# Computing, finishing and storing the last output tile of an MLP product in two column halves

## The chip, the cores and the metric

The kernel runs on one core of a Trainium2 chip. The metric is the device time of one execution in microseconds (us), the median over several executions. A profile's span is 2.1 to 2.2 us shorter than the time of the same execution (139.9 against 142.1 for the kernel before). Times inside an execution are counted from the start of that span.

## The reference, cut to what matters

```python
def _B_ref(x, w1, b1, w2, b2):
    h = _layernorm(x, axis=-1)
    u = jnp.einsum("bsd,sf->bdf", h, w1) + b1
    u = _gelu(u)
    y = jnp.einsum("bdf,fs->bds", u, w2) + b2          # the second MLP product
    return y.transpose(0, 2, 1)

h  = x + _A_ref(_layernorm(x), A_w_r, A_w_i)           # spectral filter, not touched here
h2 = h + _B_ref(_layernorm(h), B_w1, B_b1, B_w2, B_b2) # S = 2048, D = 512, F = 1376
```

The output has 2048 x 512 elements in bf16. The kernel makes it as 16 tiles of 128 x 512. Each tile needs 11 accumulating matmuls over F, one eviction by the vector engine (DVE) that adds the bias and `h`, and one store.

## The kernel before

The kernel is built by its own small scheduler: each operation is recorded with its dependences, ordered on its engine, and emitted with semaphores. Two parts matter. The first is the loop of the second product:

```python
for s2 in range(NS2):                                   # 16 tiles
    unit = PsumUnit("mm2", 1, early=True)
    for t in range(NFT):                                # 11 matmuls, the last with 96 rows
        Kt = NP if t < 10 else 96
        mm(..., lambda bank: ps[:, bank, :], W2[t][0:Kt, s2::16], GT[0:Kt, t, :], unit, ...)   # strided weights
    dst, bia, hs = OUT[:, s2, :], B2f[:, s2:s2 + 1], H[:, s2, :]
    K.op(f"fin{s2}", "dve", ... eng.scalar_tensor_tensor(dst, ps[:, bank, :], bia, hs, op0=ALU.add, op1=ALU.add), ...)
    dma(f"st_{s2}", out_psd[:, s2, :], dst, 1 << 17, ins=[dst], prio=9)
```

The second is where the instructions of each engine are emitted. `sp` is the sync engine, which issues all of the stores:

```python
def section(eng, sname=sname, ops=ops):
    last = {o.lane for o in ops[-4:]}
    for k, o in enumerate(ops):
        if sname == "sp" and k == len(ops) - 2:         # before the second-to-last DMA
            for lane in sorted(self.lane_count):
                if lane.startswith("dq") and lane not in last:
                    eng.wait_ge(sems[lane], lane_quantum(lane) * self.lane_count[lane])
        for lane, v in o.waits:
            eng.wait_ge(sems[lane], v * lane_quantum(lane))
        ins = o.emit(...)
        ...
    if sname == "sp":
        for lane in sorted(last):                       # the last four, at the end
            eng.wait_ge(...)
```

So before the second-to-last DMA of the sync engine, whichever that is, the program waits once for every DMA semaphore that is not one of the last four. The built program has 30 wait instructions there, most of them with two semaphores each. The Trainium skill describes such instructions ("Perfetto Trace Analysis", section "Identifying Dependency Chains"): an instruction that waits on several engines may have EventSemaphore instructions put in front of it. The trace has 30 such records in front of that store, 29 for the program's own waits and one with the store's wait for its eviction. I call them "the wait block".

## Time and profile before

| | kernel before |
|---|---|
| time, median | 141.94 us (141.81 to 142.0, 4 runs) |
| span of the profiled execution | 139.9 us |
| PE (matmul) busy | 122.4 us, 87% |
| last matmul over, last eviction begins | 136.74 us |
| last eviction | 0.75 us |
| last store issued, landed | 137.52, about 139.4 us |

The end of the chain of waits, the chain of work that ended last (start, duration, engine, tile or line, count):

```profile
51.34 85.38 PE ps L549 x424
136.72 0.02 issue
136.74 0.75 DVE OUT L820
```

From 51 us to the last matmul nothing but PE is on the path. Work on the tail can win at most the 3.2 us from 136.74 to the end. The timeline of the kernel before shows the evictions and stores of the last two tiles, with the store of tile 13 first (start, duration, engine, line, operation, and in brackets the engine's idle time and what ended it; SPq is the sync engine's queue):

```profile
132.76 0.33 SPq L544 DMA_DIRECT2D out_dram<-OUT  x1
...
134.36 0.75 DVE L820 SCALAR_TENSOR_TENSOR OUT<-ps,B2f,H 128x512 bf16<-128x512 f32 x1 [1.63 <-PE ps L549]
...
135.46 0.33 SPq L544 DMA_DIRECT2D out_dram<-OUT  x1
...
136.74 0.75 DVE L820 SCALAR_TENSOR_TENSOR OUT<-ps,B2f,H 128x512 bf16<-128x512 f32 x1 [1.63 <-PE ps L549]
...
137.52 0.33 SPq L544 DMA_DIRECT2D out_dram<-OUT  x1
```

The last store goes 0.03 us after its eviction ends (136.74 + 0.75 = 137.49). The store of tile 14 does not: its eviction ended at 134.36 + 0.75 = 135.11, and it went at 135.46, 0.35 us late. That small irregularity is the only sign of the wait block in the ordinary views. The raw records of the sync engine show what lies between the stores of tiles 13 and 14 (start and duration in us; this is not a view of the profile, and the comments are mine):

```
132.762 DMA   0.333     store of tile 13
133.146 EVSEM 0.017     first of 30 wait instructions
...                     (about 0.06 apart)
133.823 EVSEM 0.028
134.277 EVSEM 0.028     after a hole of 0.45
...                     (about 0.06 apart)
135.388 EVSEM 0.027     the last one
135.456 DMA   0.327     store of tile 14
```

All the semaphores in it except that of tile 14's eviction had been reached long before, so the block is not waiting for data until its very end, and even that wait (the last of the 30) finds its eviction finished. It takes 135.456 - 133.095 = 2.36 us merely to be executed. The gap between two stores is 2.38 us less the 0.33 us of an issue, so here it costs nearly nothing.

For the last store, the view of the output tile gives the time from issue to landing:

```profile
DMA to landing us min/median/max: 1.9/1.9/1.9
```

### The profile page before, as it was taken

The numbers are of one execution on the slowest core, as the hardware profiler recorded it, in microseconds if no ns is written. First come the engines' busy times: TensorE is split into PE (matmuls) and PEld (weight loads), VectorE is DVE, ScalarE is ACT, GpSimd is POOL, SyncE is SP. The second block draws the span as 40 slices with busy tenths as digits, with TensorE's granted clock in tenths as the row PEclk, the third lists the DMA queues.
The fourth block names the chain that finished last, engine by engine and source line by source line (L and its number), as shares of the span: only waits on it lengthen the run. The fifth ranks groups of instructions, "written<-read, shape, count | busy, mean of one in ns | idle before, by whom it ended". The sixth has DMA issues, their size and how long they took to land.

```text
span 139.9 us, 2050 instructions
## 1 busy us (share of the span) xinstructions
PE 122.4 (87%) x754; PEld 76.6 (55%) x754; DVE 81.3 (58%) x169; ACT 64.0 (46%) x138; POOL 18.1 (13%) x49
## 2 busy tenths in 40 slices
PE   0039779999994899999999999999999999999990
PEld 0026557677663666764444444445666666666660
DVE  0489966998597399999200779544452324242422
ACT  3699973767855599984100996533300000000000
POOL 0077700000000003667400000000000000000000
PEclk9999999999999999999999999999999999999999
DMA  4999999999999999500000000000012121212111
GB/s 125 353 391 403 343 356 335 424 415 428 422 288 348 418 274 363 205 0 0 0 5 0 0 0 0 0 0 0 0 42 75 37 75 37 75 42 75 37 49 68
DMA packets 12218, 22.77 MB, mean 163 GB/s; under 512 B 2640, under 2 KB 8784, under 8 KB 11440
## 3 DMA queue, kind: packets, MB, share of 16 engines
q1 hardware_dynamic: 11776, 21.33, 42.5%
q10 hardware_dynamic: 432, 1.31, 2.7%
q8 instruction: 6, 0.10, 0.3%
q14 instruction: 4, 0.03, 0.1%
HBM read 20.54 MB, written 2.10 MB: 162 GB/s over the span
## 4 chain that ended last, share of the span: by engine, by line
PE 75%; DVE 13%; ACT 4%; DMA 3%; POOL 2%; issue 1%; POOLq 0%
PE ps L549 75%; DVE V L712 5%; DMA X<-in_A_x_dram 3%; DVE st_94 L648 2%; POOL FS L657 2%; ACT JK L627 2%; ACT PQ L557 1%; DVE H L763 1%; DVE Y L558 1%; DVE OUT L820 1%; DVE PQ L558 1%; DVE st_101 L769 0%; ACT CS L557 0%; DVE mv_95 L650 0%; DVE FS L657 0%
## 5 line engine op out<-in xcount | busy, mean ns | idle before, releaser
L549 PE MATMUL ps<-HH,W_77 128*128 128x512 bf16 (+1 forms) x176 | 39.8, 379 | 0.2 <-DVE HH L783 0.2
L549 PEld LDWEIGHTS ps<-HH,W_77 128*128 128x128 bf16 (+1 forms) x176 | 17.6, 100 | 19.1 <-issue 0.4
L820 DVE SCALAR_TENSOR_TENSOR OUT<-ps,B2f,H 128x512 bf16<-128x512 f32 x16 | 12.0, 750 | 23.8 <-PE ps L549 23.8
L549 PE MATMUL ps<-FS,X 128*128 128x256 bf16 x64 | 9.4, 315 | 10.2 <-POOL FS L657 10.2
L549 PEld LDWEIGHTS ps<-FS,X 128*128 128x128 bf16 x64 | 6.7, 112 | 12.6 <-POOL FS L657 9.7
L763 DVE TENSOR_TENSOR H<-ps,X 128x512 bf16<-128x512 f32 x16 | 10.4, 675 | 2.2 <-PE ps L549 2.2
L549 PE MATMUL ps<-EM,V 128*128 128x128 bf16 x128 | 9.6, 220 | 1.6 <-DVE V L712 1.5
L557 ACT ACTIVATE PQ<-ps 128x512 bf16<-128x512 f32 x15 | 8.2, 598 | 6.0 <-PE ps L549 5.9
L712 DVE TENSOR_TENSOR V<-ps,Wr 128x1024 bf16<-128x1024 f32 x8 | 9.5, 1220 | 2.3 <-PE ps L549 2.3
L549 PE MATMUL ps<-EM,Y 128*128 128x256 bf16 x64 | 9.1, 273 | 1.3 <-DVE Y L558 1.0
L549 PEld LDWEIGHTS ps<-EM,V 128*128 128x128 bf16 x128 | 7.8, 98 | 3.9 <-DVE V L712 2.3
L549 PE MATMUL ps<-EM,PQ 128*128 128x256 bf16 x64 | 9.1, 272 | 0.9 <-DVE PQ L558 0.9
L712 DVE TENSOR_TENSOR V<-ps,Wi 128x1024 bf16<-128x1024 f32 x8 | 9.5, 1216 | 0.2
L557 ACT ACTIVATE EO<-ps 128x512 bf16<-128x512 f32 x16 | 8.8, 591 | 1.7 <-PE ps L549 1.5
L557 ACT ACTIVATE CS<-ps 128x512 bf16<-128x512 f32 x14 | 7.8, 606 | 3.4 <-PE ps L549 3.4
L627 ACT ACTIVATE JK<-X 128x512 bf16<-128x512 bf16 x14 | 8.6, 613 | 1.2 <-DMA X<-in_A_x_dram 1.2
L549 PE MATMUL ps<-EO,IF 128*128 128x256 bf16 (+1 forms) x48 | 9.1, 308 | 0.0
L627 ACT ACTIVATE JK<-H,nb_98 128x512 bf16<-128x512 bf16 x11 | 7.9, 719 | 2.6 <-DVE H L763 2.4
L648 DVE BATCH_NORM_STATS2 st_94<-X 128x6 f32<-128x512 bf16 x9 | 5.8, 675 | 5.0 <-DMA X<-in_A_x_dram 5.0
L549 PE MATMUL ps<-CS,EM 128*128 128x512 bf16 (+1 forms) x34 | 8.3, 367 | 0.2 <-ACT CS L557 0.2
L549 PEld LDWEIGHTS ps<-EM,Y 128*128 128x128 bf16 x64 | 5.7, 98 | 3.2 <-issue 1.2
L806 DVE TENSOR_TENSOR Q_51<-U_50 128x512 bf16<-128x512 bf16 x3 | 1.3, 423 | 10.5 <-ACT U_50 L804 10.5
(85 smaller groups left out, 194.1 us busy)
## 6 DMA issues: line engine op xcount, KB each, us to landing
W_77<-in_B_w_dram SPq DMA_DIRECT2D x4, 1376.0 KB, 14.4
out_dram<-OUT SPq DMA_DIRECT2D x16, 128.0 KB, 1.8
Wr<-in_A_w_r_dram SPq DMA_DIRECT2D x4, 257.0 KB, 4.3
Wi<-in_A_w_i_dram SPq DMA_DIRECT2D x4, 257.0 KB, 4.6
X<-in_A_x_dram SPq DMA_DIRECT2D x2, 512.0 KB, 7.1
IF<-c_IF SPq DMA_DIRECT2D x1, 1024.0 KB, 6.6
EM<-c_EM SPq DMA_DIRECT2D x1, 832.0 KB, 11.0
Wr<-in_A_w_r_dram SPq DMA_DIRECT2D x6, 128.5 KB, 5.8
```

The source lines that it names most:

```text
L549: return eng.matmul(outf(bank), lhsT, rhs, start=start, stop=stop, **({"skip_group_check": True} if skip else {}))
L557: return eng.activation(dst, srcf(bank), ACT.Copy)
L558: return eng.tensor_copy(dst, srcf(bank))
L627: K.op(name, "act", lambda s, eng, bank: eng.activation(jk, src, func, accum_out=acc, **kw), ins=[src] + ([bias] if bias is not None else ...
L648: K.op(f"ln1_st{i}", "dve", lambda s, eng, bank, st=st, i=i: eng.bn_stats(st, X[:, i, :]), ins=[X[:, i, :]], outs=[st], dur=600.0, prio=20)
L657: lambda s, eng, bank, i=i, r=r: eng.tensor_scalar(FS[:, i, :, :], FP[:, i, :, :], r, None, op0=ALU.mult),
L712: return eng.tensor_tensor(ov, src, wv, ALU.mult)
L763: K.op(f"h_{s2}", "dve", lambda s, eng, bank, xs=xs, hs=hs: eng.tensor_tensor(hs, ps[:, bank, :], xs, ALU.add), ins=[xs], outs=[hs], dur=6 ...
L806: K.op(f"gelu{t}_q", "dve", lambda s, eng, bank, U=U, Q=Q: eng.tensor_tensor(Q, U, U, ALU.mult), ins=[U], outs=[Q], dur=350.0, prio=5)
L820: K.op(f"fin{s2}", "dve", lambda s, eng, bank, dst=dst, bia=bia, hs=hs: eng.scalar_tensor_tensor(dst, ps[:, bank, :], bia, hs, op0=ALU.add ...
```

## The change

The intent is to shorten the tail behind the last matmul. With the last tile in two halves, the first half is evicted and stored while the second is being multiplied. Only a 128 x 256 eviction and a 64 KB store are then left after the last matmul.

```diff
     for s2 in range(NS2):
-        unit = PsumUnit("mm2", 1, early=True)
-        for t in range(NFT):
-            ... ps[:, bank, :], W2[t][0:Kt, s2::16], GT[0:Kt, t, :] ...
-        dst, bia, hs = OUT[:, s2, :], B2f[:, s2:s2 + 1], H[:, s2, :]
-        K.op(f"fin{s2}", "dve", ...)
-        dma(f"st_{s2}", out_psd[:, s2, :], dst, 1 << 17, ins=[dst], prio=9)
+        for d0, d1 in ((0, 512),) if s2 < NS2 - 1 else ((0, 256), (256, 512)):
+            unit = PsumUnit("mm2", 1, early=True)
+            for t in range(NFT):
+                ... ps[:, bank, 0:d1 - d0], W2[t][0:Kt, s2::16], GT[0:Kt, t, d0:d1] ...
+            dst, bia, hs = OUT[:, s2, d0:d1], B2f[:, s2:s2 + 1], H[:, s2, d0:d1]
+            K.op(f"fin{s2}_{d0}", "dve", ...)
+            dma(f"st_{s2}_{d0}", out_psd[:, s2, d0:d1], dst, (d1 - d0) * 256, ins=[dst], prio=9)
```

The order of all other instructions stays the same on every engine. One thing follows that the diff does not show: the sync engine now has one DMA more, so "before the second-to-last DMA" no longer means before the store of tile 14. It means before the first half store.

More of the change, by code (lines that the diff above doesn't have):

```diff
@@ L814, in build_kernel @@
     for s2 in range(NS2):
-        unit = PsumUnit("mm2", 1, early=True)
-        for t in range(NFT):
-            Kt = NP if t < 10 else 96
-            mm(f"mm2_{s2}_{t}", lambda bank: ps[:, bank, :], W2[t][0:Kt, s2::16], GT[0:Kt, t, :], unit, t == 0, t == NFT - 1, t == 0, 0, 512)
-        dst, bia, hs = OUT[:, s2, :], B2f[:, s2:s2 + 1], H[:, s2, :]
-        K.op(f"fin{s2}", "dve", lambda s, eng, bank, dst=dst, bia=bia, hs=hs: eng.scalar_tensor_tensor(dst, ps[:, bank, :], bia, hs, op0=ALU.add, op1=ALU.add),
-             ins=[bia, hs], outs=[dst], dur=680.0, unit=unit, pr=True, last=True, prio=5)
-        dma(f"st_{s2}", out_psd[:, s2, :], dst, 1 << 17, ins=[dst], prio=9)
+        for d0, d1 in ((0, 512),) if s2 < NS2 - 1 else ((0, 256), (256, 512)):
+            unit = PsumUnit("mm2", 1, early=True)
+            for t in range(NFT):
+                Kt = NP if t < 10 else 96
+                mm(f"mm2_{s2}_{t}", lambda bank, d0=d0, d1=d1: ps[:, bank, 0:d1 - d0], W2[t][0:Kt, s2::16], GT[0:Kt, t, d0:d1], unit, t == 0, t == NFT - 1, t == 0, 0, d1 - d0)
+            dst, bia, hs = OUT[:, s2, d0:d1], B2f[:, s2:s2 + 1], H[:, s2, d0:d1]
+            K.op(f"fin{s2}_{d0}", "dve", lambda s, eng, bank, dst=dst, bia=bia, hs=hs: eng.scalar_tensor_tensor(
+                dst, ps[:, bank, 0:dst.shape[1]], bia, hs, op0=ALU.add, op1=ALU.add),
+                ins=[bia, hs], outs=[dst], dur=(d1 - d0) / 0.96 + 150.0, unit=unit, pr=True, last=True, prio=5)
+            dma(f"st_{s2}_{d0}", out_psd[:, s2, d0:d1], dst, (d1 - d0) * 256, ins=[dst], prio=9)
     K.schedule()
```

## The prediction

> **What bounds it now.** The page gives a span of 139.9 us; PE is busy 87% of it. The chain of waits ends with one unbroken PE stretch from 51.34 us, the last eviction (DVE, 0.75 us, from 136.74), and the store of tile 15: issued at 137.52 on the sync queue (0.33 us), landed about 1.9 us after issue, then about 0.5 us to the end. So only the tail after the last matmul is at stake, 3.2 us or 2%.
>
> **What the change does.**
> - PE: the last 11 matmuls 128x512 become 22 of 128x256. The timeline spaces the wide ones 0.216 us apart; 128x256 matmuls of the first stage run 0.108 apart, so this is +0.03 us. The doubt is the strided weights: a load shows 0.144 us here against 0.098 for contiguous ones. But contiguous loads of 0.098 sustain a 0.056 us pitch, so about 0.10 us of a strided load should count, under 0.108. The Trainium skill, "TensorE: Matmul & The Clock Gate", section "LDWEIGHTS", puts a plain load at columns/1.2 ns, 107 for 128: also just hidden. If not, 22 x 0.036 = 0.8 us late.
> - DVE: 1024-wide products take 1.22 us, 512-wide 0.675: 1.06 ns per column, so the last eviction falls from 0.75 to about 0.48. Saves 0.27.
> - Store: the last has 64 KB. The 128 KB one moved its data between 138.35 and 138.9 (windows of 0.1 us); half should save 0.1 to 0.2 us of landing.
>
> Taken alone this is about -0.4 us. I do not expect to see it.
>
> **What takes it back.** The program emits its "wait for every other DMA" block before the second-to-last store, whatever that is: 30 wait instructions covering all other DMA semaphores. Before, they stand in front of store 14, where time is spare: store 13's issue ended at 133.09, store 14 went at 135.46, 0.35 us after its eviction had ended (135.11), while every other store goes 0.03 us after its own. The trace's records of the sync queue fill the gap with waits about 0.06 us apart and one hole of 0.45 us: 2.36 us in all, issue-bound, not waiting for data. The instruction order shows that after the change the same block stands between store 14 and the first half store. Now:
> - store 14 issues at 135.14, as soon as its eviction ends, done 135.47;
> - the block runs to about 137.83, although the first half was evicted near 136.07;
> - first half store 137.83 to 138.16, second from about 138.20, although its eviction ended near 137.25.
>
> The last issue moves from 137.52 to 138.20: +0.68 us. Minus about 0.13 for the smaller transfer: +0.55. The shorter PE and DVE tail is off the critical path by about 0.9 us, which also hides slow weight loads.
>
> **Prediction:** 141.95 + 0.5 = 142.45 us, range 142.1 to 142.75. Faster by over 2%: 0.005; within 2%: 0.985; slower by over 2%: 0.01.
>
> **What would show it.** Store 14 issued 0.03 us after its eviction, earlier than before; first half store over 1 us after its eviction; two half stores back to back, about 0.37 us apart, near 137.8 and 138.2; final evictions near 0.48 us; half-width matmuls about 0.108 us apart; the chain of waits ending in sync-queue issue or DMA in place of the last eviction.
>
> **What would make it wrong.** If the 0.45 us hole in the block does not recur, the last issue comes near 137.75 and the time is about 142.05. If the waits pass quicker still, it could fall to 141.6. If the second half store has to queue behind the first, or lands slower with 512-byte rows, it is 142.7 or more. Strided loads costing over 1 us in all would show only beyond that slack.

## The result, and the profile after

| | before | changed |
|---|---|---|
| time, median | 141.94 us (4 runs) | 142.53 us (142.37 to 142.66, 4 runs) |
| ratio to before | | 1.0043 (95% interval 1.0025 to 1.006) |
| span of the profiled execution | 139.9 us | 140.4 us |

The change is 0.6 us slower. That is far inside the 2% that counts as "same", but clear of the noise.

The end of the chain of waits of the changed kernel:

```profile
133.71 3.02 PE ps L549 x24
136.76 0.48 DVE OUT L821
```

The last eviction begins at 136.76 in place of 136.74. Counted from the eviction of tile 14 in each execution it begins 2.41 us later (136.76 - 134.34, in the timeline below) in place of 2.38 (136.74 - 134.36), so twenty-two half-width matmuls cost PE about 0.03 us, as foreseen. The last eviction itself is 0.48 in place of 0.75 us. Up to here the intent was met, and the work of the engines is over at 137.24 in place of 137.49. The timeline shows what follows (eviction and store of tile 14, eviction of the first half, eviction of the second, the two half stores):

```profile
134.34 0.75 DVE L821 SCALAR_TENSOR_TENSOR OUT<-ps,B2f,H 128x512 bf16<-128x512 f32 x1 [1.63 <-PE ps L549]
...
135.13 0.33 SPq L544 DMA_DIRECT2D out_dram<-OUT  x1
...
135.55 0.48 DVE L821 SCALAR_TENSOR_TENSOR OUT<-ps,B2f,H 128x256 bf16<-128x256 f32 x1 [0.45 <-PE ps L549]
...
136.76 0.48 DVE L821 SCALAR_TENSOR_TENSOR OUT<-ps,B2f,H 128x256 bf16<-128x256 f32 x1 [0.72 <-PE ps L549]
...
137.81 0.34 SPq L544 DMA_DIRECT2D out_dram<-OUT  x1
...
138.20 0.42 SPq L544 DMA_DIRECT2D out_dram<-OUT  x1
```

The first half has been ready since 135.55 + 0.48 = 136.03 and is issued at 137.81, 1.8 us later. The second has been ready since 137.24 and goes at 138.20, right behind the first. The raw records of the sync engine fill the time:

```
135.127 DMA   0.332     store of tile 14
135.510 EVSEM 0.017     first of 30 wait instructions
...
136.117 EVSEM 0.028
136.568 EVSEM 0.028     after the hole of 0.45
...
137.740 EVSEM 0.028     the last one
137.806 DMA   0.337     first half store
138.201 DMA   0.419     second half store
```

It is the same block with the same length (137.81 - 135.46 = 2.35 us), one store later. The time from issue to landing of the two half stores, from the view of the output tile:

```profile
DMA to landing us min/median/max: 1.6/1.6/1.6
```

This is the sum on the profiled execution: the last store is issued 0.68 us later (137.52 to 138.20), and it lands faster by 0.21 (1.86 to 1.65 from the records). The span grows by 0.46 us. The medians differ by 0.59. Of the 0.68, the block alone makes 0.28: the first half store goes at 137.806, where the whole one went at 137.522. The other 0.40 is the second half store, which now has to go behind the first (0.395 us from one issue to the next).

### The profile page after: what moved, and what is told of

Its sections match the earlier page's. It is cut to its first block, busy times and chain, and to the rows that moved or that the text cites. A ratio compares the mean times of both kernels' runs of the same rounds, so it can differ in the third digit from the quotient of the medians.

```text
span 140.4 us, 2065 instructions
## 1 busy us (share of the span) xinstructions
PE 121.5 (87%) x756; PEld 77.5 (55%) x765; DVE 81.4 (58%) x170; ACT 64.1 (46%) x138; POOL 18.1 (13%) x49
## 4 chain that ended last, share of the span: by engine, by line
PE 75%; ACT 10%; DVE 8%; DMA 3%; issue 1%
PE ps L549 75%; ACT JK L627 6%; DVE V L712 5%; DMA X<-in_A_x_dram 3%; ACT PQ L557 1%; ACT sd L619 1%; DVE st L648 1%; DVE Y L558 1%; ACT EO L557 1%; ACT Y L557 1%; DVE PQ L558 1%; DVE H L763 0%; ACT CS L557 0%; DVE OUT L821 0%; DVE mv L650 0%
## 5 line engine op out<-in xcount | busy, mean ns | idle before, releaser
L549 PE MATMUL ps<-HH,W 128*128 128x512 bf16 (+1 forms) x171 | 39.0, 379 | 0.2
L549 PE MATMUL ps<-GT,W 128*128 128x512 bf16 (+3 forms) x183 | 38.1, 366 | 0.2
L549 PEld LDWEIGHTS ps<-GT,W 128*128 128x128 bf16 (+1 forms) x187 | 26.2, 144 | 12.1 <-issue 0.2
L549 PEld LDWEIGHTS ps<-HH,W 128*128 128x128 bf16 (+1 forms) x176 | 17.6, 100 | 19.1 <-issue 0.4
L821 DVE SCALAR_TENSOR_TENSOR OUT<-ps,B2f,H 128x512 bf16<-128x512 f32 (+1 forms) x17 | 12.2, 720 | 23.3 <-PE ps L549 23.3
L804 ACT ACTIVATE U<-ps,B1f 128x512 bf16<-128x512 f32 (+1 forms) x11 | 7.2, 684 | 12.6 <-PE ps L549 12.6
L806 DVE TENSOR_TENSOR Q<-U 128x512 bf16<-128x512 bf16 (+1 forms) x11 | 4.5, 420 | 12.8 <-ACT U L804 12.8
L810 ACT ACTIVATE SG<-P 128x512 bf16<-128x512 bf16 (+1 forms) x11 | 6.7, 626 | 6.9 <-DVE P L809 6.9
```

The source lines that it names most:

```text
L549: return eng.matmul(outf(bank), lhsT, rhs, start=start, stop=stop, **({"skip_group_check": True} if skip else {}))
L804: K.op(f"gelu{t}_u", "act", lambda s, eng, bank, U=U, bia=bia, Mt=Mt: eng.activation(U, ps[0:Mt, bank, :], ACT.Identity, bias=bia, scale=1.0),
L806: K.op(f"gelu{t}_q", "dve", lambda s, eng, bank, U=U, Q=Q: eng.tensor_tensor(Q, U, U, ALU.mult), ins=[U], outs=[Q], dur=350.0, prio=5)
L810: K.op(f"gelu{t}_sg", "act", lambda s, eng, bank, P2=P2, SG=SG: eng.activation(SG, P2, ACT.Sigmoid, scale=2.0 * GELU_C), ins=[P2], outs=[S ...
L821: K.op(f"fin{s2}_{d0}", "dve", lambda s, eng, bank, dst=dst, bia=bia, hs=hs: eng.scalar_tensor_tensor(dst, ps[:, bank, 0:dst.shape[1]], bi ...
```

## The experiments

There were two theories. **Theory W**: the wait block holds back both half stores, and the halves themselves are worth what they were meant to be worth. **Rival R**: the halves themselves cost, through half-width matmuls with strided weight loads or through two short stores; the waits had been in the program before at no cost, so they are no cause. All results were correct. Each "before" below is the kernel before in the same rounds.

| kernel | split | wait block | time, median | before | ratio, 95% interval |
|---|---|---|---|---|---|
| changed kernel | all | before first half store | 142.53 | 141.94 | 1.0043 (1.0025 to 1.006) |
| split_early | all | six stores earlier | 141.53 | 142.06 | 0.9963 (0.995 to 0.9976) |
| whole_early | none | six stores earlier | 142.04 | 142.06 | 0.9997 (0.9984 to 1.001) |
| store_split_only | store | before first half store | 142.99 | 142.06 | 1.0064 (1.005 to 1.0077) |
| compute_split_only | matmuls, evictions | before store of tile 14 | 141.76 | 142.06 | 0.9979 (0.9966 to 0.9993) |
| whole_late | none | before the last store | 143.18 | 142.11 | 1.0085 (1.0066 to 1.0103) |
| split_half | all | half of it earlier | 141.54 | 142.11 | 0.9964 (0.9952 to 0.9976) |
| split_double | all | twice as long | 144.37 | 142.11 | 1.0162 (1.0149 to 1.0176) |
| split_384_128_early | 384 + 128 | six stores earlier | 141.47 | 142.11 | 0.9957 (0.9944 to 0.997) |
| whole_late_pad | none | before the last store | 142.33 | 142.05 | 1.0015 (0.9984 to 1.0045) |
| store_split_only_pad | store | before first half store | 142.63 | 142.05 | 1.0036 (1.0005 to 1.0067) |
| whole_pad | none | before store of tile 14 | 142.06 | 142.05 | 1.0002 (0.9963 to 1.0041) |

### split_early: the change with the block out of the way

```diff
-                    if sname == "sp" and k == len(ops) - 2:
+                    if sname == "sp" and k in (len(ops) - 8, len(ops) - 2):
                         for lane in sorted(self.lane_count):
-                            if lane.startswith("dq") and lane not in last:
+                            if lane.startswith("dq") and lane not in last and (lane in {o.lane for o in ops[-10:]}) == (k == len(ops) - 2):
```

No wait is dropped. Those whose DMA was issued long ago are executed six stores earlier, and only three wait instructions stay in the old place.

> The changed kernel with 27 of its 30 wait instructions moved six stores earlier; the same waits in all. Theory W (the block of waits on the sync queue holds back both half stores): first half store issues near 136.1, second near 137.28, 0.03 us after its eviction; time about 141.55 us, 0.4 under the kernel before and 1.0 under the changed one. Rival R (the halves themselves cost: half-width matmuls with strided weight loads, two short stores with 512-byte rows): the waits were there before at no cost, moving them changes nothing, time stays about 142.5.

Measured: 141.53 us, 0.5 under the kernel before. The timeline of split_early (evictions of the two halves and their stores):

```profile
135.48 0.48 DVE L821 SCALAR_TENSOR_TENSOR OUT<-ps,B2f,H 128x256 bf16<-128x256 f32 x1 [0.45 <-PE ps L549]
136.69 0.48 DVE L821 SCALAR_TENSOR_TENSOR OUT<-ps,B2f,H 128x256 bf16<-128x256 f32 x1 [0.72 <-PE ps L549]
...
136.06 0.33 SPq L544 DMA_DIRECT2D out_dram<-OUT  x1
...
137.20 0.33 SPq L544 DMA_DIRECT2D out_dram<-OUT  x1
```

The second half store now goes 0.03 us after its eviction. The same matmuls, evictions and stores that made a kernel of 142.53 us make one of 141.53. R falls as the explanation of the loss.

### whole_early: the same move without the split

The edit is that of split_early, on the kernel before.

> The kernel before, undivided, with the same waits moved six stores earlier. Theory W: store 14 issues 0.03 us after its eviction in place of 0.35, but the last store is still issued at 137.52, so the time stays within 0.1 us of 141.94. If the placing of the waits were worth something of its own, this kernel would be faster by 0.3 us or more and the gain of split_early would not be the split's.

Measured: 142.04 against 142.06 us, ratio 0.9997. Moving the block is worth nothing by itself, because the last store was not behind it. The timeline of whole_early has the store of tile 14 at 135.22, after an eviction that ended at 135.13. That is 0.09 us and not the 0.03 that I had written, since the eviction's own wait still stands in a separate wait instruction. The last store:

```profile
137.53 0.33 SPq L544 DMA_DIRECT2D out_dram<-OUT  x1
```

So the gain of split_early is the split's, and the loss of the changed kernel is the block's.

### store_split_only: two half stores, nothing else split

```diff
-        dma(f"st_{s2}", out_psd[:, s2, :], dst, 1 << 17, ins=[dst], prio=9)
+        for d0, d1 in ((0, 512),) if s2 < NS2 - 1 else ((0, 256), (256, 512)):
+            dma(f"st_{s2}_{d0}", out_psd[:, s2, d0:d1], OUT[:, s2, d0:d1], (d1 - d0) * 256, ins=[OUT[:, s2, d0:d1]], prio=9)
```

> The kernel before with whole matmuls and one whole last eviction; only its last store is cut in two. Theory W: the extra store puts the block of waits behind store 14; first half store near 137.83, second near 138.20 as in the changed kernel, time about 142.5. Rival R, in the form that the half-width matmuls cost it: about 141.95 to 142.1. Rival R, in the form that two short stores cost it: 142.5 as well, but with the first half store issued at 137.52.

Measured: 142.99 us. Adding one DMA instruction is enough to bring the loss. In the timeline of store_split_only the whole eviction ends at 136.62 + 0.75 = 137.37, and the first half store is issued at 137.71, 0.34 us later and 2.36 after the issue of tile 14's store had ended:

```profile
135.02 0.33 SPq L544 DMA_DIRECT2D out_dram<-OUT  x1
...
137.71 0.33 SPq L544 DMA_DIRECT2D out_dram<-OUT  x1
```

The form of R in which two short stores cost it foresaw the first half store at the kernel's old 137.52 (here, with an eviction that ended 0.12 earlier, at about 137.40). But the time is about 0.5 us more than theory W had said, so something else is in it. The half stores took 2.0 and 2.2 us to land in place of the changed kernel's 1.6. This is taken up under whole_late.

### compute_split_only: half matmuls and evictions, one store

```diff
-            dma(f"st_{s2}_{d0}", out_psd[:, s2, d0:d1], dst, (d1 - d0) * 256, ins=[dst], prio=9)
+        dma(f"st_{s2}", out_psd[:, s2, :], OUT[:, s2, :], 1 << 17, ins=[OUT[:, s2, :]], prio=9)
```

> Half-width matmuls and two half evictions, but one whole last store, so the block of waits stays in front of store 14 as in the kernel before. Theory W: last store issued near 137.28 in place of 137.52, time about 141.7 (0.24 under the kernel before). Rival R, half-width matmuls cost it: 142.2 or more.

Measured: 141.76 us, 0.3 under the kernel before (0.24 foreseen). With one store fewer the block is back in front of tile 14's store. The timeline of compute_split_only, second eviction and last store:

```profile
136.65 0.48 DVE L821 SCALAR_TENSOR_TENSOR OUT<-ps,B2f,H 128x256 bf16<-128x256 f32 x1 [0.72 <-PE ps L549]
...
137.16 0.33 SPq L544 DMA_DIRECT2D out_dram<-OUT  x1
```

The half-width matmuls cost 0.03 us again (2.41 us between the starts of tile 14's eviction and the last), and the shorter eviction gains about what it was costed at. split_early gains about 0.2 us more (0.9963 against 0.9979), and the smaller last store lands in 1.6 us where the whole one here takes 1.8. The two intervals overlap, so the share of the store is not settled by times alone.

### whole_late: no split at all, only the block one store later

```diff
-                    if sname == "sp" and k == len(ops) - 2:
+                    if sname == "sp" and k == len(ops) - 1:
```

> The kernel before, undivided, with the block of 30 waits moved one store later, directly in front of the last store; nothing is split. Theory W: store 14 issues at 135.14 and the block runs 2.36 us from 135.47, so the last store issues near 137.83 in place of 137.52 and the time is about 142.25 to 142.3, 0.3 over the kernel before. If the block only costs where a store is split (Rival R), the time stays at 142.0.

Measured: 143.18 us, slower than the kernel before by 1.1 us. The direction is that of theory W. The timeline of whole_late has the last store where it was foreseen, 0.34 us after its eviction ended:

```profile
136.78 0.75 DVE L820 SCALAR_TENSOR_TENSOR OUT<-ps,B2f,H 128x512 bf16<-128x512 f32 x1 [1.63 <-PE ps L549]
...
137.88 0.33 SPq L544 DMA_DIRECT2D out_dram<-OUT  x1
```

The block's place costs a kernel that splits nothing, too. But the size is wrong: 0.3 us had been foreseen. The view of the output tile shows where the rest is, the time from issue to landing of the last store:

```profile
DMA to landing us min/median/max: 2.4/2.4/2.4
```

The view of windows of whole_late, 0.1 us each, shows the last store's data. The columns are the window, then busy times of the engines, then the granted clock, the DMA engines' mean busy share and GB/s:

```profile
138.90:139.00 0.10, 0.00 (x0) 0.00 (x0) 0.00 (x0) 0.00 (x0) 0.00 (x0) 1.00 1.01 358
139.00:139.10 0.10, 0.00 (x0) 0.00 (x0) 0.00 (x0) 0.00 (x0) 0.00 (x0) 1.00 0.79 267
139.10:139.20 0.10, 0.00 (x0) 0.00 (x0) 0.00 (x0) 0.00 (x0) 0.00 (x0) 1.00 0.19 52
139.20:139.30 0.10, 0.00 (x0) 0.00 (x0) 0.00 (x0) 0.00 (x0) 0.00 (x0) 1.00 0.00 0
139.30:139.40 0.10, 0.00 (x0) 0.00 (x0) 0.00 (x0) 0.00 (x0) 0.00 (x0) 1.00 0.09 31
139.40:139.50 0.10, 0.00 (x0) 0.00 (x0) 0.00 (x0) 0.00 (x0) 0.00 (x0) 1.00 0.08 10
139.50:139.60 0.10, 0.00 (x0) 0.00 (x0) 0.00 (x0) 0.00 (x0) 0.00 (x0) 1.00 0.08 10
139.60:139.70 0.10, 0.00 (x0) 0.00 (x0) 0.00 (x0) 0.00 (x0) 0.00 (x0) 1.00 0.06 10
```

After 139.2 no data move for 0.1 us, and from 139.3 on a share of 0.06 to 0.09 goes on, about one engine of the sixteen. The raw DMA records suggest what kept it: an 8 KB packet of an instruction queue starts at 138.70 and takes 0.615 us, to 139.31. The last eight 1 KB packets of the store, one sixteenth of its 128, start only then, the first at 139.31. The last store's 16 completions are written by 139.21, except one, at 139.84. store_split_only has such a packet too, at 138.55, and its last completion is 0.22 us after the one before. In the traces of the kernels with half evictions no such packet comes after 137.4; they have one near 103.4 in its place. This is "theory F", tested next.

The Trainium skill has the parts of this picture ("DMA: Bandwidth & Descriptors", section "Queues, rings and completion order"): each DMA engine takes turns between its queues in whole packets, and row 14 is the runtime's own, refills among its uses. The trace fits this: the eight packets wait until the whole 0.615 us packet is done. The page of the profile lists the queue in part 3 as "q14 instruction", with four packets.

### whole_late_pad, store_split_only_pad, whole_pad: shifting the DVE program by one instruction

The changed kernel has one DVE instruction more than the undivided ones. Each of these kernels gets one too, a one-column fill of an unused cell at the start. The order of all other instructions stays the same.

```diff
+    K.op("pad", "dve", lambda s, eng, bank: eng.memset(EPS[:, 3:4], 0.0), outs=[EPS[:, 3:4]], dur=60.0, prio=40)
     K.op("half", "pool", ...)
```

> whole_late was 0.9 us slower than foreseen although its last store was issued at 137.88, as foreseen. Its trace has an 8 KB packet of the instruction queue from 138.70 for 0.6 us in the midst of the last store, and one of the 16 completions came 0.64 us after the others. This kernel is whole_late with one tiny DVE instruction more at the start, to shift the DVE program by one instruction, as the changed kernel does (in its trace, and in all with half evictions, that packet comes at about 103.4 instead). Theory F (the instruction fetch delays the last store): packet gone from 138.7, landing 1.7 to 1.9 us after issue, time about 142.35. If the packet is harmless: 143.2 again.

Measured: 142.33 us; without the pad it was 143.18. The two ratios to the kernel before, 1.0015 and 1.0085, have intervals that do not overlap. The packet is at 103.28 and no longer near 138.7. The view of the output tile of whole_late_pad:

```profile
DMA to landing us min/median/max: 1.8/1.8/1.8
```

The medians now give +0.28 us over the kernel before for the block's place alone, where 0.3 had been foreseen. One slower run on each side widens the interval of the ratio so that it includes 1, so this size rests on the medians and on the issue times.

> store_split_only with the same extra DVE instruction. Theory F: packet gone from 138.55, second half store still issued near 138.1 to 138.2 and landing 1.6 us later in place of 2.0, time about 142.55, that of the changed kernel. If the packet is harmless: 143.0 again.

Measured: 142.63 us, where it was 142.99; the packet is at 103.17; the half stores land 1.6 to 1.7 us after issue. That is the changed kernel's loss (0.58 over the kernel before by the medians, against 0.59) from one DMA instruction alone. The intervals of the two ratios overlap a little here, so for this pair the verdict rests on the landing as well.

> The kernel before with the same extra DVE instruction, as a control: its packet at 138.81 comes when the last store's data have nearly all moved, so theory F expects 141.9 to 142.05, within 0.15 us of the kernel before. Clearly faster (141.7 or less) would mean that part of the gain of the half evictions in the other runs is the packet's moving and not the shorter tail.

Measured: 142.06 against 142.05 us. By the medians the control holds: the pad is worth nothing where the packet came at 138.81, when the store's data had nearly all moved. One slower run on each side (142.53 and 142.86) makes the interval of this ratio wide, 0.9963 to 1.0041, so the interval alone would not exclude a gain as large as split_early's. The traces show a small effect: the last store lands 1.77 us after issue in whole_pad, and 1.86 and 1.96 in the profiles of the kernel before and of whole_early, which have the late packet. So, by an estimate from these single profiles, 0.1 to 0.2 us of the gains of the split kernels can be the packet's moving. The loss of the changed kernel against split_early is free of this question, since neither has a packet this late.

### split_half: half of the block moved

```diff
-                        for lane in sorted(self.lane_count):
-                            if lane.startswith("dq") and lane not in last:
+                        for j, lane in enumerate(sorted(self.lane_count)):
+                            if lane.startswith("dq") and lane not in last and (lane in {o.lane for o in ops[-10:]} or j % 2 == 0) == (k == len(ops) - 2):
```

Here too `k` takes both places, as in split_early.

> The changed kernel with 14 of its 30 wait instructions moved six stores earlier and 16 left in front of the first half store. Theory W says the block costs only what sticks out past the last eviction: 16 waits of 0.06 us from 135.47 end at 136.45 (136.85 with a hole of 0.4), the first half store goes there, the second still at 137.28, time about 141.55, the same as with all waits moved. If the cost were simply in proportion to the waits left late, the time would be about 142.05 (halfway between 141.53 and 142.53).

Measured: 141.54 us, all of split_early's gain. The timeline of split_half:

```profile
136.35 0.33 SPq L544 DMA_DIRECT2D out_dram<-OUT  x1
...
137.13 0.33 SPq L544 DMA_DIRECT2D out_dram<-OUT  x1
```

The first half store is held back by 0.46 us (its eviction ended at 135.90), the second by 0.03. The sixteen late waits end before the second half is ready, so they are free. The cost is not in proportion to the waits; only what sticks out past the last eviction counts.

### split_double: the block twice

```diff
-                        for lane in sorted(self.lane_count):
+                        for lane in sorted(self.lane_count) * 2:
```

> The changed kernel with every wait of the block given twice (59 wait instructions in place of 30, all on semaphores long reached). Theory W: 29 more instructions of 0.062 us, +1.8 us on the issue of both half stores and on the time: about 144.3 (144.7 if a second hole of 0.4 us appears). If the block waited for a transfer to land, giving the waits twice would add nothing: 142.5.

Measured: 144.37 us, 1.84 over the changed kernel by the medians of different rounds. The timeline of split_double has both half stores together:

```profile
139.70 0.81 SPq L544 DMA_DIRECT2D out_dram<-OUT  x2
```

In the raw records the issue of tile 14's store ends at 135.586, so the block of 59 instructions takes 139.698 - 135.586 = 4.11 us. The 29 more of them cost 4.112 - 2.347 = 1.765 us, or 0.061 each, although every semaphore they ask for had been reached. The waits are paid for being executed, not for waiting.

### split_384_128_early: what a strided weight load costs

```diff
-        for d0, d1 in ((0, 512),) if s2 < NS2 - 1 else ((0, 256), (256, 512)):
+        for d0, d1 in ((0, 512),) if s2 < NS2 - 1 else ((0, 384), (384, 512)):
```

It has the edit of split_early as well.

> The kernel split_early with the last tile cut into 384 and 128 columns. It measures what a strided weight load costs when the matmul is too short to hide it: if a load occupies about 0.10 us as the prediction estimated, the last 11 matmuls of 128 columns come 0.10 us apart, the products take 0.5 us longer, the last eviction is 0.13 shorter and the time is about 141.9 (0.35 over split_early). If only 0.056 us as for contiguous loads, the time is about 141.4.

Measured: 141.47 us. The last eleven matmuls in the trace, each with its own strided weight load, start 0.059 to 0.072 us apart, mostly 0.061 to 0.064, where matmuls of 128 columns with contiguous weights run 0.056 apart in an earlier stage. So at most about 0.06 us of a strided load counts here, and not 0.10. In the view of groups by shape, of split_384_128_early, the matmuls are as follows (ten of each; the eleventh has 96 rows and its own group; the means, 326 and 227 ns, are how long one is under way, and the matmuls overlap):

```profile
L549 PE MATMUL ps<-GT,W 128*128 128x384 bf16 x10 | 1.8, 326 | 0.0
L549 PE MATMUL ps<-GT,W 128*128 128x128 bf16 x10 | 0.8, 227 | 0.0
```

The time is no better than that of split_early, within the noise: the last eviction is 0.35 us, 0.13 shorter, but it begins at 136.82 in place of 136.69, and the second store goes at 137.21 in place of 137.20. split_early and this one are both faster than the kernel before and the changed kernel. The gain of 0.4% is small, but its interval excludes 1. split_early is the version I would keep.

## Why the prediction was right

The prediction was right: 142.45 us foreseen, in 142.1 to 142.75, and 142.53 measured. It was right because the instruction order was read together with the diff, and because the 0.35 us delay of one store in the kernel before was followed up. One part was assumed and not derived: that the hole of 0.45 us in the block would come again. It did, but by the prediction's own reckoning the time without it would have been about 142.05, just outside the range. Point by point:

- *The block moves in front of the first half store and takes 2.36 us.* It did: 2.35 us, hole included. Half stores foreseen at 137.83 and 138.20 were issued at 137.81 and 138.20. split_early shows that without it the change gains 0.5 us, store_split_only_pad that one more DMA is enough for the loss (0.28 by the block's place, as in whole_late_pad, and the rest by a second store behind the first), and split_double that each wait costs 0.061 us.
- *The half eviction takes about 0.48 us and matmuls come 0.108 us apart.* It took 0.48 us. The matmuls start 0.108 to 0.113 us apart. The Trainium skill's formula ("TensorE: Matmul & The Clock Gate", section "Back-to-back issue gap"), N/2.4 + 2.5 ns for isolated matmuls, gives 109 ns for 256 columns, and the trace agrees (most starts are 0.108 to 0.110 us apart).
- *The smaller store saves about 0.13 us.* Landing fell by 0.21 in the profiled pair (1.86 to 1.65). Not all of this is the size: the kernel before had the late instruction packet at 138.81, and whole stores with no such packet near them landed in 1.77 us (compute_split_only, whole_late_pad, whole_pad). Against these the saving is 0.12, about as foreseen. A half store that does not follow right behind another lands in 1.57 us (split_early), a saving of 0.20.
- *"About 0.10 us of a strided load should count."* This step failed, without harm: the load had only to be under 0.108. The formula in the page's section "LDWEIGHTS" gives 107 ns for 128 columns, and split_384_128_early shows loads 0.06 us apart. The same page's section "Weight-path perf modes" says that loads of 128 non-FP32 columns go about twice as fast, strided ones included; the trace, with starts 0.06 us apart, agrees with that one.
- *"The chain of waits ending in sync-queue issue or DMA."* This sign did not appear. The chain still ends in the last eviction at 136.76, although the program was held by the sync engine. That view does not count wait instructions. The delay shows only as the 0.96 us between the end of the eviction and the issue of its store.
- *Slow weight loads would be hidden by 0.9 us of slack.* Not tested, as they were not slow. The slack was 138.20 - 137.24 = 0.96 us.

Left open: what the hole of 0.45 us in the block is. It lies after the tenth wait in the changed kernel and after the eleventh in the kernel before, so at the same instruction of the sync program; in split_early, with the block six stores earlier, the hole moved along, to 122.6. An 8 KB instruction packet begins about 0.6 us after it ends (at 137.20 and 134.90; at 123.22 in split_early), which suggests that the sequencer stops to ask for more of its program. Nothing here tests that. Nor is it known what the late packet that delayed whole_late brings. The pad shows only that its time depends on the length of the DVE program.

## What to carry to other kernels

When a change adds an instruction to a queue, look at what else the program places by counting from that queue's end: here a harmless block of waits moved from a gap into the tail, and it cost more than the change could gain. A wait for something long finished is not free; count the wait instructions in front of the last store, and execute them where that queue has spare time. Check a costed saving at the queue that ends the program, not only at the engine that was shortened, since the chain of waits need not show the queue's waits at all.

## What the Trainium skill lacked or had wrong

- "Perfetto Trace Analysis", section "Identifying Dependency Chains", names the extra EventSemaphore instructions but gives no cost. On the sync engine, one on reached semaphores costs 0.061 us (29 more of them, 1.765 us).
- "TensorE: Matmul & The Clock Gate", section "LDWEIGHTS", has a formula that gives 107 ns for a load of 128 columns, with no word there of the fast load. Strided bf16 loads sustained starts 0.06 us apart here.
- The same page, section "Back-to-back issue gap", gives a sustained 81 ns per matmul at 128 columns and 131 at 512. Streams of load and matmul pairs here ran at 56 ns (contiguous weights) and 216 ns, as its formula for isolated ones says.
- No page says that an instruction fetch can delay a kernel's last store; "Runtime: NRT & Kernel Launch", section "Instruction fetch mechanics", where it would belong, lacks it. In whole_late one 8 KB packet of 0.6 us put one of 16 completions 0.64 us behind the others, and one more DVE instruction took 0.85 us off the median of that kernel (143.18 to 142.33).
